# A decode attention block: key and value tiles of four heads and 8 MB in three buffers, in place of two heads and 4 MB in five

## The chip, the cores and the metric

The kernel runs on one core of a Trainium2 chip. The metric is the device time of one execution in microseconds, as the median of several runs. Beside it there is a profile of one execution, with the span from the first to the last instruction.

## The reference

A block with adaptive layer norm: attention of one new token per sequence over a cache of 4096 keys and values in 32 heads, then a feed-forward part. All arrays are float32; the two caches have 268 MB each.

```python
B, D, H, Sk, Dh, F = 4, 512, 32, 4096, 128, 1792
mod = (silu(c) @ w_mod).reshape(4, 6, 1, -1)            # shifts, scales and gates sa, ca, ga, sb, cb, gb
h = layernorm(x) * (1 + ca) + sa
q = (h @ wq) split into 32 heads                        # B, H, 1, Dh
p = softmax(einsum("bhqd,bhkd->bhqk", q, k_cache) * Dh ** -0.5)
o = einsum("bhqk,bhkd->bhqd", p, v_cache)
x = x + ga * (o.reshape(B, 1, H * Dh) @ wo)
h = layernorm(x) * (1 + cb) + sb
return x + gb * (silu(h @ w1) @ w2)
```

## The kernel before

The work on the caches goes in N = 64 steps `n`, one for each of 16 pairs of heads (`t`) and each of 4 sequences (`b`). A step has one K tile and one V tile of 4 MB: two heads (`HP` = 2), each spread over 64 partitions (`HALF`), with 64 consecutive cache rows (`NJ`), that is 32 KB in one piece of the cache, on each partition. All large loads are issued by SyncE (SP) through `fetch` (L71), in program order, into five buffers of 32 KB per partition (pool `kv`, `bufs=5`) that are reused in turn. The order of instructions on each engine is that of the program (a manual schedule). A load waits on SP until the last reader of its buffer's old tile is done, and the loads behind it wait with it.

Step n, by engine:

- `mult` (L216): GpSimd multiplies the first `NA` = 24 of the 64 rows of a partition by the query, in place, with the query's copy `qw` in SBUF; VectorE does the other 40 with the query `qb` in PSUM.
- `red` (L221), VectorE: sums each row's 128 products to a score; first the 40 rows, then the 24 of GpSimd.
- `rowmax` (L225), VectorE; `bmax` (L229), a transpose on TensorE that spreads the maxima over the partitions; `negmax` (L236), VectorE, per head.
- `softexp` (L247), ScalarE: exponentials, one instruction per head, written into the zero-padded tile `pz` at distances of 32 columns, and their sum into `rs`.
- `pv` (L260), TensorE: 16 products of four cache rows at a time with the exponentials, added up in PSUM tile `po`. Each is issued in two passes (x2 in the instruction counts), and so are the other float32 products.

Once in four steps, `make_qb` (L202, L210) spreads the queries of a head pair over the partitions by products with `ident` columns, and `finish_a` and `finish_b` (L269 to L285) copy `po` to SBUF, gather the values by 16 products with columns of `sel`, and divide by the sum of the exponentials; the result goes into `oz`.

Before the steps come the modulation (`mods`, L146), the first layer norm and the queries (L186), whose weights `wm` and `wq` pass through the same five buffers. After the steps come the output projection (`project`, L294), the second layer norm (L161 to L173), and the feed-forward products (L352, L362). Their weights `wo`, `w1` and `w2` follow the last tiles through the buffers, cut into several loads. In the last four steps the loads stand in an order of their own, written by hand: K61, K62, K63, V61, V62, the first half of `wo`, V63, the second half of `wo`, `w1`, `w2`.

Of the kernel before, what the change touches and what calls it, by code (L numbers as in the profile page):

```python
# [17 lines left out]
def kernel(  # L18
# [20 lines left out]
    HP = 2  # L39
    HALF = P // HP  # L40
# [3 lines left out]
    NG = NJ // JJ  # L44
    NK = D // P
    NI = F // P
    FG = F // G
    NA = 24
# [3 lines left out]
    NP = 3  # L52

    const = ctx.enter_context(tc.tile_pool(name="const", bufs=1))
    kv = ctx.enter_context(tc.tile_pool(name="kv", bufs=5))
# [7 lines left out]
    wmv = wm.rearrange("(p k) n -> p k n", p=P)  # L63
    wqv = wq.rearrange("(p k) n -> p k n", p=P)
    wov = wo.rearrange("(t p j) n -> p t j n", p=P, j=HP)
    w1v = w1.rearrange("(p k) f -> p k f", p=P)
    w2v = w2.rearrange("(p i) d -> p i d", p=P)
# [31 lines left out]
    wmt = [load(f"wm{i}", [P, 2, 6 * D], wmv[:, 2 * i : 2 * i + 2, :]) for i in range(2)]  # L99
    wqt = [load(f"wq{i}", [P, 2, H * Dh], wqv[:, 2 * i : 2 * i + 2, :]) for i in range(2)]  # L100
# [4 lines left out]
    blk = const.tile([P, P], F32, name="blk")  # L105
    nc.vector.memset(blk, 0.0)
    for i in range(HP):
        nc.vector.memset(blk[HALF * i : HALF * (i + 1), HALF * i : HALF * (i + 1)], 1.0)
# [12 lines left out]
    oz = const.tile([P, NT, HP, W], F32, name="oz")
    nc.gpsimd.memset(oz, 0.0)

    def silu2(dst, src, n):
        t = work.tile([P, FG], F32, tag="silu", name="silu", bufs=1)
        nc.scalar.activation(t[:, :n], src, AF.Tanh, scale=0.5)
        nc.vector.scalar_tensor_tensor(dst, t[:, :n], 1.0, src, op0=ALU.add, op1=ALU.mult)

    def transposed(src, m, name):
        d = const.tile([P, m, W], F32, name=name)  # L130
        nc.vector.transpose(d, src.rearrange("p (c k) -> p k c", k=m))  # L131
        return d

    cs = const.tile([P, P], F32, name="cs")
    silu2(cs, cg, P)
    csT = transposed(cs, NK, "csT")
    mod = const.tile([P, 6, P], F32, name="mod")
    sa, ca1, ga, sb, cb1, gb = (mod[:, i, :] for i in range(6))

    def mods(i, m):  # L140
# [34 lines left out]
    mods(0, 2)  # L175
    hg = const.tile([P, P], F32, name="hg")
    layernorm_mod(hg, xg, sa, ca1)
    hT = transposed(hg, NK, "hT")
    mods(2, 4)

    CW = 4 * Dh
    pq = [psum([P, CW], "q", 2) for _ in range(2)]
    for k in range(NK):
        for ch in range(H * Dh // CW):
            i, g = divmod(ch, G)
            nc.tensor.matmul(  # L186
                pq[i][W * g : W * (g + 1), :], hT[:, k, :], wqt[k // 2][:, k % 2, ch * CW : (ch + 1) * CW],
                start=k == 0, stop=k == NK - 1,
            )
    qs = const.tile([P, 2, CW], F32, name="qs")  # L190
    for i in range(2):
        nc.scalar.activation(qs[:, i, :], pq[i], AF.Copy, scale=SCALE)

    qb, qw = {}, {}

    def make_qb(t):
        p = psum([P, B, Dh], "q", 2)
        for b in range(B):
            for i in range(HP):
                ch, u = divmod(HP * t + i, CW // Dh)  # L200
                j, g = divmod(ch, G)
                nc.tensor.matmul(  # L202
                    p[HALF * i : HALF * (i + 1), b, :],
                    ident[:, W * g + b : W * g + b + 1].to_broadcast([P, HALF]),
                    qs[:, j, u * Dh : (u + 1) * Dh],
                    start=True, stop=True,
                )
        qb[t] = p
        qw[t] = work.tile([P, B, Dh], F32, tag="qw", name=f"qw{t}")
        nc.scalar.activation(qw[t], p, AF.Copy)  # L210

    sc, nm, po, rs, sm = {}, {}, {}, {}, {}

    def mult(eng, src, n, lo, hi):
        t, b = divmod(n, B)
        eng.tensor_mul(  # L216
            kt[n][:, lo:hi, :], kt[n][:, lo:hi, :], src[t][:, b : b + 1, :].to_broadcast([P, hi - lo, Dh])
        )
# [4 lines left out]
    def rowmax(n):  # L223
        nm[n] = work.tile([P, 1], F32, tag="rm", name=f"rm{n}", bufs=3)
# [7 lines left out]
    def negmax(n):  # L232
        t = work.tile([P, 1], F32, tag="nm", name=f"nm{n}", bufs=3)
        for i in range(HP):
            h = slice(HALF * i, HALF * (i + 1))
            nc.vector.tensor_reduce(t[h], nm[n][h, h], axis=AX.X, op=ALU.max, negate=True)  # L236
        nm[n] = t

    def softexp(n):
        t, b = divmod(n, B)  # L240
        if b == 0:
            rs[t] = work.tile([P, B], F32, tag="rs", name=f"rs{t}", bufs=3)
        o = W // 2 - JJ
        for i in range(HP):
            h = slice(HALF * i, HALF * (i + 1))
            w = pz[n % NP][h, : NG * W].rearrange("p (g w) -> p g w", w=W)
            nc.scalar.activation(  # L247
                w[:, :, o + i * W // 2 : o + i * W // 2 + JJ],
                sc[n][h].rearrange("p (g j) -> p g j", j=JJ),
                AF.Exp, bias=nm[n][h], accum_out=rs[t][h, b : b + 1],  # L250
            )

    def pv(n):
        t, b = divmod(n, B)
        if b == 0:
            po[t] = psum([P, JJ * Dh], "po", 2)
        o = W // 2 - JJ - JJ * b
        for j in range(NG):
            g = j % G
            nc.tensor.matmul(  # L260
                po[t][W * g : W * (g + 1), :],
                pz[n % NP][:, j * W + o : (j + 1) * W + o],
                vt[n][:, JJ * j : JJ * (j + 1), :].rearrange("p j d -> p (j d)"),
                start=(b == 0 and j < G), stop=(b == B - 1 and j >= NG - G),
            )

    def finish_a(t):
        o = work.tile([P, JJ, Dh], F32, tag="o", name="o")
        nc.vector.tensor_copy(o, po[t].rearrange("p (j d) -> p j d", j=JJ))  # L269
        d = psum([P, 1 + HP, B], "small", 1)  # L270
        nc.tensor.matmul(d[:, 0, :], blk, rs[t], start=True, stop=True)
        for i in range(HP):
            for r in range(HP):
                for j in range(JJ):
                    s = i * W // 2 + j
                    nc.tensor.matmul(  # L276
                        d[HALF * i : HALF * (i + 1), 1 + r, :], o[:, j, r::HP], sel[:, s : s + JJ * (B - 1) + 1 : JJ],
                        start=j == 0, stop=j == JJ - 1,
                    )
        sm[t] = d  # L280

    def finish_b(t):
        rd = work.tile([P, 1, B], F32, tag="rd", name="rd")
        nc.vector.reciprocal(rd, sm[t][:, 0:1, :])
        nc.vector.tensor_mul(oz[:, t, :, :B], sm[t][:, 1 : 1 + HP, :], rd.to_broadcast([P, HP, B]))  # L285

    accp = psum([P, P], "acc", 1)
    wot = []

    def project(lo, hi):  # L290
        for t in range(lo, hi):
            for r in range(HP):
                for g in range(G):
                    nc.tensor.matmul(  # L294
                        accp[W * g : W * (g + 1), :], oz[:, t, r, :],
                        wot[t // NH][:, t % NH, r, g * P : (g + 1) * P],
                        start=(t == 0 and r == 0), stop=(t == NT - 1 and r == HP - 1),
                    )
# [98 lines left out]
```

## Time and profile before

| | |
|---|---|
| runs | 1332.4, 1333.32, 1333.3 us; median 1333.3 us |
| profiled execution | 1334.54 us, its span 1332.5 us |
| granted TensorE clock, mean | 0.656 |
| bytes moved by DMA | 567.87 MB, mean 426 GB/s over the span |
| busy: VectorE, TensorE, GpSimd, ScalarE | 976.2, 504.9, 435.2, 75.7 us |

The profile is of one execution. A busy TensorE counts pipelined products that overlap, so the sum of their durations is larger than its busy time. DMA share is the mean busy share of the core's 16 DMA engines; in short stretches it can come out somewhat above 1, since a packet's time and bytes are counted where the packet lies by its start or end. In lines of groups, the columns are line, engine, operation, tiles written and read with their shapes, count, busy time in us and mean ns of one, and then the idle time before them with what ended it. In lines of the timeline and of the chain, the first number is the start in us, the second the duration. In the stretches view the columns are the stretch, its length, the busy time of TensorE, its weight load, VectorE, ScalarE and GpSimd, each with a count of instructions in brackets, and last the granted clock, the DMA share and GB/s.

### The profile page before, as it was taken

The page shows a single profiled execution, that of the slowest core. Times are in us where ns is not written, and L with a number is a line of the kernel's source. Part 1 is how long each engine was busy: PE and PEld are TensorE (multiplying, and loading weights), DVE is VectorE, ACT ScalarE, POOL GpSimd, SP SyncE. Part 2 cuts the span into 40 slices and gives each one's busy share as a digit, 9 for nine tenths or more (in the row PEclk, how much of TensorE's full clock was granted, in tenths as well). Part 3 has the DMA queues.
Part 4 walks back from the last instruction along what each step waited for, and adds up shares of the span by engine and source line. Part 5 has one row for each costly group of instructions (what it writes and reads, how often), then busy time and mean ns, then how long its engine had stood idle before and what let it go on. Part 6 is the DMA issues. An engine that isn't in the chain of part 4 may idle for free.

```text
span 1332.5 us, 8833 instructions
## 1 busy us (share of the span) xinstructions
PE 504.9 (38%) x3576; PEld 181.2 (14%) x3576; DVE 976.2 (73%) x468; ACT 75.7 (6%) x289; POOL 435.2 (33%) x79
## 2 busy tenths in 40 slices
PE   3244324433442533443343233334333333433157
PEld 2011101110110111101011110101111011101024
DVE  1487787788778778777877877777787787778851
ACT  1100000000000000000000000000000000000000
POOL 1244234324323423432442343243234234324600
PEclk9666677666656666656666676576666556666677
DMA  9999999999999999999999999999999999999997
GB/s 407 427 430 433 426 436 428 429 435 426 433 432 429 433 427 435 430 430 432 427 435 429 428 434 429 432 430 431 432 429 430 430 432 432 431 428 433 431 414 288
DMA packets 22376, 567.87 MB, mean 426 GB/s; under 512 B 2448, under 2 KB 2496, under 8 KB 5056
## 3 DMA queue, kind: packets, MB, share of 16 engines
q1 hardware_dynamic: 22160, 567.29, 99.3%
q8 instruction: 28, 0.46, 0.1%
q14 instruction: 12, 0.10, 0.0%
q0 software_dynamic: 128, 0.01, 0.0%
q10 hardware_dynamic: 48, 0.01, 0.0%
HBM read 567.30 MB, written 0.01 MB: 426 GB/s over the span
## 4 chain that ended last, share of the span: by engine, by line
DMA 48%; DVE 35%; PE 10%; issue 4%; ACT 2%; DVEq 0%; ACTq 0%
DMA k<-in_A_k_cache_dram 45%; DVE sc L221 20%; DVE k L216 13%; PE po L260 8%; DMA v<-in_A_v_cache_dram 2%; ACT pz L247 2%; PE mx L229 1%; DMA wm<-in_w_mod_dram 1%; DVE o L269 1%; DVE rm L225 1%; DVE nm L236 1%; PE acc L294 0%; PE po L362 0%; PE q L352 0%; DVE oz L285 0%
## 5 line engine op out<-in xcount | busy, mean ns | idle before, releaser
L216 POOL TENSOR_TENSOR k<-k,qw 128x3072 f32<-128x3072 f32 x64 | 429.7, 6715 | 827.9 <-DMA k<-in_A_k_cache_dram 786.7
L221 DVE TENSOR_REDUCE sc<-k 128x40 f32<-128x5120 f32 (+1 forms) x128 | 560.8, 4413 | 5.2
L216 DVE TENSOR_TENSOR k<-k,q 128x5120 f32<-128x5120 f32 x64 | 351.2, 5488 | 245.9 <-DMA k<-in_A_k_cache_dram 188.2
L260 PE MATMUL po<-v,pz 128*32 128x512 f32 x2048 | 371.5, 892 | 103.0 <-ACT pz L247 77.1
L229 PE MATMUL mx<-ident,rm 128*128 128x128 f32 x64 | 28.5, 445 | 641.4 <-DVE rm L225 641.4
L260 PEld LDWEIGHTS po<-v,pz 128*32 128x32 f32 x2048 | 82.6, 155 | 349.0 <-issue 256.3
L247 ACT ACTIVATE pz<-sc,nm 64x64 f32<-64x64 f32 x128 | 44.2, 345 | 1054.1 <-DVE nm L236 1052.5
L229 PEld LDWEIGHTS mx<-ident,rm 128*128 128x128 f32 x64 | 11.6, 181 | 676.2 <-issue 648.2
L236 DVE TENSOR_REDUCE nm<-mx 64x1 f32<-64x64 f32 x128 | 28.4, 222 | 45.9 <-PE mx L229 43.9
L276 PE MATMUL small<-sel,o 128*64 128x4 f32 x512 | 43.0, 231 | 46.6 <-DVE o L269 46.6
L276 PEld LDWEIGHTS small<-sel,o 128*64 128x64 f32 x512 | 41.6, 190 | 48.0 <-DVE o L269 48.0
L247 ACT ACTIVATION_READ_ACCUMULATOR pz<-sc,nm 64x1 f32 x128 | 23.6, 185 | 0.0
L269 DVE COPY o<-po 128x512 f32<-128x512 f32 x16 | 11.0, 684 | 16.2 <-PE po L260 16.2
L202 PE MATMUL q<-qs,ident 128*64 128x128 f32 x256 | 17.5, 279 | 0.0
L225 DVE TENSOR_REDUCE rm<-sc 128x1 f32<-128x64 f32 x64 | 14.1, 220 | 2.2
L202 PEld LDWEIGHTS q<-qs,ident 128*64 128x64 f32 x256 | 13.6, 136 | 14.5 <-issue 14.5
L210 ACT ACTIVATE qw<-q 128x512 f32<-128x512 f32 x16 | 9.6, 597 | 105.5 <-PE q L202 105.5
L146 PE MATMUL q<-wm,csT 128*32 128x128 f32 x192 | 7.5, 322 | 17.2 <-DVE csT L131 13.5
L186 PE MATMUL q<-wq,hT 128*32 128x512 f32 x64 | 10.1, 790 | 9.5 <-DMA wq<-in_A_wq_dram 9.5
L294 PE MATMUL acc<-wo,oz 128*32 128x128 f32 x256 | 11.7, 369 | 0.4 <-DMA wo<-in_A_wo_dram 0.4
L294 PEld LDWEIGHTS acc<-wo,oz 128*32 128x32 f32 x256 | 11.2, 154 | 0.7 <-issue 0.6
L146 PEld LDWEIGHTS q<-wm,csT 128*32 128x32 f32 x192 | 6.2, 129 | 17.9 <-DVE csT L131 13.5
(57 smaller groups left out, 63.8 us busy)
## 6 DMA issues: line engine op xcount, KB each, us to landing
k<-in_A_k_cache_dram SPq DMA_DIRECT2D x64, 4096.0 KB, 36.0
v<-in_A_v_cache_dram SPq DMA_DIRECT2D x64, 4096.0 KB, 30.3
wq<-in_A_wq_dram SPq DMA_DIRECT2D x2, 4096.0 KB
wm<-in_w_mod_dram SPq DMA_DIRECT2D x2, 3072.0 KB, 10.1
wo<-in_A_wo_dram SPq DMA_DIRECT2D x1, 4096.0 KB
wo<-in_A_wo_dram SPq DMA_DIRECT2D x1, 2048.0 KB
w<-in_B_w_dram SPq DMA_DIRECT2D x1, 2048.0 KB, 23.7
w<-in_B_w_dram SPq DMA_DIRECT2D x1, 1792.0 KB
```

The costliest lines, as they stand in the source:

```text
L146: nc.tensor.matmul(p[W * g : W * (g + 1), u, :], csT[:, k, :], wmt[k // 2][:, k % 2, o : o + P], start=k == 0, stop=k == NK - 1,)
L202: nc.tensor.matmul(p[HALF * i : HALF * (i + 1), b, :], ident[:, W * g + b : W * g + b + 1].to_broadcast([P, HALF]), qs[:, j, u * Dh : (u + ...
L216: eng.tensor_mul(kt[n][:, lo:hi, :], kt[n][:, lo:hi, :], src[t][:, b : b + 1, :].to_broadcast([P, hi - lo, Dh]))
L221: nc.vector.tensor_reduce(sc[n][:, lo:hi], kt[n][:, lo:hi, :], axis=AX.X, op=ALU.add)
L225: nc.vector.tensor_reduce(nm[n], sc[n], axis=AX.X, op=ALU.max)
L229: nc.tensor.transpose(p, nm[n].to_broadcast([P, P]), ident)
L236: nc.vector.tensor_reduce(t[h], nm[n][h, h], axis=AX.X, op=ALU.max, negate=True)
L247: nc.scalar.activation(w[:, :, o + i * W // 2 : o + i * W // 2 + JJ], sc[n][h].rearrange("p (g j) -> p g j", j=JJ), AF.Exp, bias=nm[n][h], ...
L260: nc.tensor.matmul(po[t][W * g : W * (g + 1), :], pz[n % NP][:, j * W + o : (j + 1) * W + o], vt[n][:, JJ * j : JJ * (j + 1), :].rearrange ...
L269: nc.vector.tensor_copy(o, po[t].rearrange("p (j d) -> p j d", j=JJ))
L276: nc.tensor.matmul(d[HALF * i : HALF * (i + 1), 1 + r, :], o[:, j, r::HP], sel[:, s : s + JJ * (B - 1) + 1 : JJ], start=j == 0, stop=j == ...
L294: nc.tensor.matmul(accp[W * g : W * (g + 1), :], oz[:, t, r, :], wot[t // NH][:, t % NH, r, g * P : (g + 1) * P], start=(t == 0 and r == 0 ...
```

## The change

A step now takes four heads (`HP` = 4) of one sequence, on 32 partitions each (`QW`): N = 32 steps with a K and a V tile of 8 MB, with 128 cache rows and 64 KB in one piece per partition. There are three buffers of 64 KB per partition. Of the 128 rows GpSimd multiplies 56 (`NA`), VectorE 72.

- Loads: K(n+1) is issued at the head of step n, V(n+1) behind `softexp(n)`; near the end the order is K30, K31, V30, V31, `wo`, `w1` and `w2`. `wm` and `wq` are one load each, and `wo` has runs of 8 KB. Small tiles of the start (among them `cg`, `qs` and the selecting matrix `zsel`) share the first buffer with `wm`, and small tiles of the end share the last one with `w1` and `w2`.
- Queries: eight products with shifted views of `zsel` put the 32 pairs of head group and sequence into one tile `qn`; `make_qb` runs in each step: ScalarE masks `qn` by a column of `sel`, one product with the block matrix `blk` spreads it, ScalarE copies it to SBUF.
- Exponentials: one ScalarE instruction for all four heads, in place; then two GpSimd products with the head mask `hm` spread them into `pz` (two half tiles in place of three whole ones).
- `negmax`: a maximum per head, a product with the negative head mask, and a sum.
- `pv`: 32 products; `po` serves two sequences, so there are two `po` tiles per head group.
- Values: `gather` masks `po` by `jm` on VectorE and adds up four products with the selecting matrix `spick`, after two and after four sequences; `norm` forms the reciprocal sums on TensorE and VectorE; `spread` divides, transposes on VectorE and copies into `oz`.
- End: the projection is interleaved with the last `gather` and `spread`, and small products `busy` without use stand on TensorE between the products of the feed-forward part.

The core of the diff:

```diff
-    HP = 2
-    HALF = P // HP
+    HP = 4
+    QW = P // HP
...
-    NA = 24
+    NA = 56
...
-    kv = ctx.enter_context(tc.tile_pool(name="kv", bufs=5))
+    kv = ctx.enter_context(tc.tile_pool(name="kv", bufs=3))
...
+    def load(dst, cache, name, n):
+        t, b = divmod(n, B)
+        dst[n] = Slot(f"{name}{n}").take(NJ, Dh)
+        src = cache[b, HP * t : HP * (t + 1)].rearrange("h (p j) d -> (h p) j d", p=QW)
+        nc.sync.dma_start(dst[n], src)
...
-    wov = wo.rearrange("(t p j) n -> p t j n", p=P, j=HP)
+    wov = wo.rearrange("(t p r) n -> p t r n", p=P, r=R)
...
+    s0 = Slot("wm")
+    wmt = s0.take(NK, 6 * D)
+    cg, cs, hg0, sa, ca1 = (s0.take(P) for _ in range(5))
...
+    qs = s0.take(2, CW)
+    zsel = s0.take(ZB + P)
...
+    pqn = psum([P, Dh], "mx", 2)
+    for i in range(2):
+        for u in range(HP):
+            o = ZB - QW * u - G * B * i
+            nc.tensor.matmul(
+                pqn, zsel[:, o : o + P], qs[:, i, u * Dh : (u + 1) * Dh],
+                start=i + u == 0, stop=i == 1 and u == HP - 1,
+            )
+    qn = const.tile([P, Dh], F32, name="qn")
+    nc.scalar.activation(qn, pqn, AF.Copy)
...
+    def make_qb(n):
+        m = work.tile([P, Dh], F32, tag="lnu", name=f"qm{n}", bufs=1)
+        nc.scalar.activation(m, qn, AF.Copy, scale=sel[:, n : n + 1])
+        p = psum([P, Dh], "q", 2)
+        nc.tensor.matmul(p, blk.rearrange("p i x -> p (i x)"), m, start=True, stop=True)
+        qb[n] = p
+        qw[n] = work.tile([P, Dh], F32, tag="qw", name=f"qw{n}")
+        nc.scalar.activation(qw[n], p, AF.Copy)
...
+        m = work.tile([P, HP], F32, tag="hx", name=f"hx{n}")
+        nc.vector.tensor_reduce(m, nm[n].rearrange("p (i x) -> p i x", i=HP), axis=AX.X, op=ALU.max)
+        nc.vector.tensor_mul(m, m, hn)
+        nm[n] = work.tile([P, 1], F32, tag="nm", name=f"nm{n}")
+        nc.vector.tensor_reduce(nm[n], m, axis=AX.X, op=ALU.add)
...
+        nc.scalar.activation(sc[n], sc[n], AF.Exp, bias=nm[n], accum_out=rs[t][:, b : b + 1])
+        for h in range(2):
+            nc.gpsimd.tensor_mul(
+                pz[h][:, : HG * W].rearrange("p (g x) -> p g x", g=HG)[:, :, E:].rearrange("p g (i j) -> p g i j", i=HP),
+                sc[n][:, HG * JJ * h : HG * JJ * (h + 1)].rearrange("p (g j) -> p g j", j=JJ)
+                .unsqueeze(2).to_broadcast([P, HG, HP, JJ]),
+                hm.unsqueeze(1).unsqueeze(3).to_broadcast([P, HG, HP, JJ]),
+            )
...
+    def gather(t, q):
+        o = work.tile([P, JJ, Dh], F32, tag="o", name="o", bufs=1)
+        nc.vector.tensor_mul(
+            o, po[t, q].rearrange("p (j d) -> p j d", j=JJ), jm.unsqueeze(2).to_broadcast([P, JJ, Dh])
+        )
+        if q == 0:
+            od[t] = psum([P, Dh], "od", 1)
+        for j in range(JJ):
+            nc.tensor.matmul(
+                od[t], spick[:, 2 - 2 * q : 2 - 2 * q + P], o[:, j, :],
+                start=(q == 0 and j == 0), stop=(q == 1 and j == JJ - 1),
+            )
...
+    def spread(t):
+        on = work.tile([P, R, QW], F32, tag="lnu", name="on", bufs=1)
+        nc.vector.tensor_scalar(
+            on, od[t].rearrange("p (x r) -> p r x", r=R), rd[t][:, 1:2], None, op0=ALU.mult
+        )
+        ot = work.tile([P, R, W], F32, tag="ot", name="ot", bufs=1)
+        nc.vector.transpose(ot, on)
+        nc.vector.tensor_copy(oz[:, t], ot[:, :, :B])
...
     for n in range(N):
         t, b = divmod(n, B)
-        if n + 1 < N - 3:
+        if n + 1 < N - 1:
             load_k(n + 1)
-            load_v(n + 1)
...
+        elif n == N - 2:
+            load_v(n)
         else:
-            load_v(n)
-            wot.append(load("wo1", [P, NH, HP, D], wov[:, NH:], 0, NH // 2, 3 * NH // 4, NH - 1, NH))
+            so = Slot("wo")
+            wot = so.take(NT, R, D)
+            fetch(wot, wov, 0, NT // 2, NT - 2, NT - 1, NT)
...
         mult(nc.gpsimd, qw, n, 0, NA)
         mult(nc.vector, qb, n, NA, NJ)
+        if n + 1 < N:
+            make_qb(n + 1)
         red(n, NA, NJ)
+        if n and b == 0:
+            gather(t - 1, 1)
+        if b == 2:
+            gather(t, 0)
         red(n, 0, NA)
+        if n and b == 0:
+            spread(t - 1)
         rowmax(n)
         bmax(n)
         negmax(n)
         softexp(n)
+        if n < N - 3:
+            load_v(n + 1)
+        elif n == N - 3:
+            load_k(N - 1)
+        elif n == N - 2:
+            load_v(N - 1)
+        else:
+            s2 = Slot("w12")
+            w1t = s2.take(NK, F)
+            w2t = s2.take(NI, D)
+            fetch(w1t, w1v, 0, 2, 3, 4)
+            fetch(w2t, w2v, 0, 4, 8, 11, 13, 14)
+        if b == B - 1:
+            norm(t)
         pv(n)
+    project(0, NT // 2)
+    gather(NT - 1, 1)
+    project(NT // 2, NT - 1)
+    spread(NT - 1)
+    project(NT - 1, NT)
...
+    busy(4)
     layernorm_mod(hg, x1, sb, cb1)
-    h2T = transposed(hg, NK, "h2T")
+    transposed(h2T, hg, NK)
+    busy(5)
```

More of the change, by code (lines that the diff above doesn't have):

```diff
@@ L98 @@
         nc.gpsimd.dma_start(xg[W * g : W * g + B, :], xr[:, g * P : (g + 1) * P])
-    wmt = [load(f"wm{i}", [P, 2, 6 * D], wmv[:, 2 * i : 2 * i + 2, :]) for i in range(2)]
-    wqt = [load(f"wq{i}", [P, 2, H * Dh], wqv[:, 2 * i : 2 * i + 2, :]) for i in range(2)]
+    nc.sync.dma_start(wmt, wmv)
+    s1 = Slot("wq")
+    wqt = s1.take(NK, H * Dh)
+    nc.sync.dma_start(wqt, wqv)
     load_k(0)
@@ L104 @@
     make_identity(nc, ident)
[L105 to L108, printed above, removed]
+    i4 = ident.rearrange("p (i x) -> p i x", i=G)
     epst = const.tile([P, 1], F32, name="epst")
@@ L111 @@
     sel = const.tile([P, W], F32, name="sel")
-    nc.vector.tensor_add(sel, ident[:, 0:W], ident[:, W : 2 * W])
-    for g in range(2, G):
-        nc.vector.tensor_add(sel, sel, ident[:, W * g : W * (g + 1)])
+    nc.vector.tensor_reduce(sel, ident.rearrange("p (g x) -> p x g", g=G), axis=AX.X, op=ALU.add)
     avg = const.tile([P, G, W], F32, name="avg")
@@ L117 @@
         nc.vector.tensor_scalar(avg[:, g, :], sel, 1.0 / G, None, op0=ALU.mult)
-    pz = [const.tile([P, NG * W + W // 2], F32, name=f"pz{i}") for i in range(NP)]
+    hm = const.tile([P, HP], F32, name="hm")
+    nc.vector.tensor_reduce(hm, i4, axis=AX.X, op=ALU.add)
+    hn = const.tile([P, HP], F32, name="hn")
+    nc.vector.tensor_scalar(hn, hm, -1.0, None, op0=ALU.mult)
+    jm = const.tile([P, JJ], F32, name="jm")
+    nc.vector.tensor_reduce(jm, ident.rearrange("p (k j) -> p j k", j=JJ), axis=AX.X, op=ALU.add)
@@ new lines @@
+    xm = const.tile([P, B], F32, name="xm")
+    nc.vector.tensor_copy(xm, sel[:, 0:B])
+    pad = const.tile([P, 1], F32, name="pad")
+    nc.vector.tensor_reduce(pad, sel[:, B:W], axis=AX.X, op=ALU.add)
+    nc.vector.tensor_add(xm[:, 0:1], xm[:, 0:1], pad)
+    blk = const.tile([P, HP, QW], F32, name="blk")
+    nc.vector.tensor_copy(blk, hm.unsqueeze(2).to_broadcast([P, HP, QW]))
+    spick = const.tile([P, P + 2], F32, name="spick")
+    nc.vector.memset(spick, 0.0)
+    ia = ident.rearrange("p (g a i j) -> p a i g j", g=G, a=2, i=HP)
@@ L119 @@
+    sp3 = spick[:, 2:].rearrange("p (i x) -> p i x", i=HP)
+    for a in range(2):
+        nc.vector.tensor_reduce(sp3[:, :, a], ia[:, a], axis=AX.XY, op=ALU.add)
+    pz = [const.tile([P, HG * W + E], F32, name=f"pz{i}") for i in range(2)]
     for t in pz:
         nc.gpsimd.memset(t, 0.0)
[L121 to L140, printed above, removed]
+    oz = const.tile([P, NT, R, B], F32, name="oz")
+    nc.vector.memset(zsel, 0.0)
@@ new lines, with silu2, transposed @@
+    nc.vector.tensor_copy(zsel[:, ZB:P].rearrange("p (g x) -> p g x", g=G), i4[:, :, :B])
+    def silu2(dst, t, src):
+        nc.scalar.activation(t, src, AF.Tanh, scale=0.5)
+        nc.vector.scalar_tensor_tensor(dst, t, 1.0, src, op0=ALU.add, op1=ALU.mult)
+    def transposed(dst, src, m):
+        nc.vector.transpose(dst, src.rearrange("p (c k) -> p k c", k=m))
+    silu2(cs, tmp, cg)
+    transposed(csT, cs, NK)
+    mod = const.tile([P, 4, P], F32, name="mod")
+    ga, sb, cb1, gb = (mod[:, i, :] for i in range(4))
@@ L141, in mods @@
+    def mods(dsts, i):
         p = psum([P, 4, P], "q", 2)
-        for u in range(m):
+        for u in range(len(dsts)):
             for k in range(NK):
@@ L223, in rowmax @@
     def rowmax(n):
[L224 removed]
+        nm[n] = work.tile([P, 1], F32, tag="rm", name=f"rm{n}")
         nc.vector.tensor_reduce(nm[n], sc[n], axis=AX.X, op=ALU.max)
@@ L241, in softexp @@
         if b == 0:
[L242 to L250, printed above, removed]
+            rs[t] = work.tile([P, B], F32, tag="rs", name=f"rs{t}")
+        nc.scalar.activation(sc[n], sc[n], AF.Exp, bias=nm[n], accum_out=rs[t][:, b : b + 1])
[5 more added lines that the diff above has]
+                hm.unsqueeze(1).unsqueeze(3).to_broadcast([P, HG, HP, JJ]),
             )
@@ L263, in pv @@
                 vt[n][:, JJ * j : JJ * (j + 1), :].rearrange("p j d -> p (j d)"),
-                start=(b == 0 and j < G), stop=(b == B - 1 and j >= NG - G),
+                start=(a == 0 and j < G), stop=(a == 1 and j >= NG - G),
             )
[L267 to L285, printed above, removed]
+    od = {}
+    def gather(t, q):
[10 more added lines that the diff above has]
+            )
@@ new lines, with norm @@
+    rd = {}
+    def norm(t):
+        p = psum([P, B], "mx", 2)
+        nc.tensor.matmul(p, blk.rearrange("p i x -> p (i x)"), rs[t], start=True, stop=True)
+        m = work.tile([P, B], F32, tag="dx", name="dx")
+        nc.vector.tensor_mul(m, p, xm)
+        rd[t] = work.tile([P, 2], F32, tag="rd", name="rd")
+        nc.vector.tensor_reduce(rd[t][:, 0:1], m, axis=AX.X, op=ALU.add)
+        nc.vector.reciprocal(rd[t][:, 1:2], rd[t][:, 0:1])
+    def spread(t):
[6 more added lines that the diff above has]
+        nc.vector.tensor_copy(oz[:, t], ot[:, :, :B])
@@ L332, with busy @@
         softexp(n)
-        if n == N - 1:
-            w1t = load("w1", [P, NK, F], w1v, 0, 2, 3, 4)
-            w2t = load("w2", [P, NI, D], w2v, 0, 8, 12, 13, 14)
-            project(0, NH)
-        pv(n)
-        if b == 1 and t + 1 < NT:
-            make_qb(t + 1)
-    finish_a(NT - 1)
-    finish_b(NT - 1)
-    project(NH, NT)
-    x1 = const.tile([P, P], F32, name="x1")
+        if n < N - 3:
[12 more added lines that the diff above has]
+            norm(t)
+        pv(n)
+    project(0, NT // 2)
[3 more added lines that the diff above has]
+    project(NT - 1, NT)
+    idle = psum([P, P], "q", 2)
+    def busy(m):
+        for _ in range(m):
+            nc.tensor.matmul(idle, ident, qn, start=True, stop=True)
+    x1, hg, y = (s2.take(P) for _ in range(3))
+    h2T, hid, th, hidT = s2.take(NK, W), s2.take(FG), s2.take(FG), s2.take(NI, W)
     nc.vector.tensor_mul(x1, ga, accp)
     nc.vector.tensor_add(x1, x1, xg)
+    busy(4)
     layernorm_mod(hg, x1, sb, cb1)
-    h2T = transposed(hg, NK, "h2T")
+    transposed(h2T, hg, NK)
+    busy(5)
     ph = psum([P, FG], "q", 2)
@@ L355 @@
             )
-    hid = const.tile([P, FG], F32, name="hid")
-    silu2(hid, ph, FG)
-    hidT = transposed(hid, NI, "hidT")
+    busy(6)
+    silu2(hid, th, ph)
+    transposed(hidT, hid, NI)
     pf = psum([P, P], "po", 2)
```

123 lines of the change are left out of this document (48 added, 75 removed).

## The prediction

> **What bounds the kernel now.** First the page's engine totals, the 40-slice strip and the DMA lines, then the two longest waits of SP.
>
> ```profile
> span 1332.5 us, 8833 instructions
> PE 504.9 (38%) x3576; PEld 181.2 (14%) x3576; DVE 976.2 (73%) x468; ACT 75.7 (6%) x289; POOL 435.2 (33%) x79
> DMA  9999999999999999999999999999999999999997
> DMA packets 22376, 567.87 MB, mean 426 GB/s; under 512 B 2448, under 2 KB 2496, under 8 KB 5056
> q1 hardware_dynamic: 22160, 567.29, 99.3%
> k<-in_A_k_cache_dram SPq DMA_DIRECT2D x64, 4096.0 KB, 36.0
> v<-in_A_v_cache_dram SPq DMA_DIRECT2D x64, 4096.0 KB, 30.3
> ...
> SPq L71 <- DVE rm L225: 719.5, 63, 15.5
> SPq L71 <- PE po L260: 464.9, 61, 9.5
> ```
>
> The DMA engines are busy in every slice, 99.3% of the span on SP's queue alone. VectorE has 73% of the span, no other engine more than 38%. A K tile lands 36.0 us after its issue, while one tile's data passes in about 9.7 us, so three transfers or more always stand in the queue. What SP waits for (719.5 us on VectorE, 464.9 us on TensorE) is only that queue being full. So I look for what makes the DMA engines' own work shorter, and then at the two ends of the span, where the queue can run dry.
>
> Packets, from the stretches view. The second row is almost all from `wo`, whose runs are 4 KB, the third likewise; the first is K and V alone, in 32 KB runs. Its last two columns are DMA share and GB/s.
>
> ```profile
> 60.00:1260.00 1200.00, 443.52 (x2764) 146.43 (x2764) 930.23 (x417) 64.45 (x264) 418.99 (x63) 0.64 1.00 431
> 1276.00:1279.00 3.00, 2.12 (x12) 0.74 (x16) 2.89 (x2) 0.00 (x0) 0.00 (x0) 0.66 1.01 406
> 1301.00:1304.00 3.00, 3.00 (x20) 0.84 (x16) 0.00 (x0) 0.00 (x0) 0.00 (x0) 0.50 1.05 424
> ```
>
> The 22160 packets add up as one packet for each contiguous run: 16384 of K and V (128 transfers x 128 partitions), 3456 of the weights, 2304 completion writes (144 loads x 16 engines), 16 for the output's data and completions. No run up to 32 KB is cut. Rate over share is 431 GB/s for 32 KB runs, and 406/1.01 = 402 and 424/1.05 = 404 for 4 KB ones. With 16 engines a 32 KB packet takes 32768 x 16 / 431 = 1216 ns, a 4 KB one 65536 / 403 = 162.6 ns. A line through both has a slope of 0.03675 ns per byte and 12 ns per packet that don't depend on size (11 to 13 by the rounding of the shares).
>
> **The change part by part.**
>
> *K and V in 64 KB runs.* Bytes stay; if the 64 KB run is one packet, it takes 65536 x 0.03675 + 12 = 2420 ns in place of 2 x 1216. An engine now handles 16384/16 = 1024 such packets; 512 fall away, 512 x 12 = **-6.1 us** (-5.6 to -6.7). Bound from the other side: 0, if the run is cut in two. I take one packet, by the count above. 64 fewer transfers also save 64 completion writes per engine, between 0 and 12 ns each: **-0.4 us**. `wo` goes from 4 KB to 8 KB runs: 64 packets less per engine, -0.8 us; `wm` in one piece and two extra cuts of `w2` cancel.
>
> The Trainium skill (SBUF — State Buffer, The DMA setup-cost knee) puts one DMA at 2 us plus bytes over 436 GB/s; by that, 64 DMAs fewer would save 128 us and the sum would be near 1205 us. The trace disagrees: K and V run at 431 GB/s without gaps, so that fixed cost lies under the queued transfers.
>
> *Three buffers.* Counting allocations, K(n+1) takes the place of V(n-1), and V(n+1) that of K(n), so V(n+1) can be issued only when K(n) has been reduced. Does the queue hold? Rows of instructions by form, then the first and the last regular K tile from the chain, and two groups of `pv` from the timeline:
>
> ```profile
> L216 POOL TENSOR_TENSOR k<-k,qw 128x3072 f32<-128x3072 f32 x64 | 429.7, 6715 | 827.9 <-DMA k<-in_A_k_cache_dram 786.7 <-issue 41.2
> L260 PE MATMUL po<-v,pz 128*32 128x512 f32 x2048 | 371.5, 892 | 103.0 <-ACT pz L247 77.1 <-DMA v<-in_A_v_cache_dram 21.9 <-issue 4.0
> L216 DVE TENSOR_TENSOR k<-k,q 128x5120 f32<-128x5120 f32 x64 | 351.2, 5488 | 245.9 <-DMA k<-in_A_k_cache_dram 188.2 <-issue 57.6
> L221 DVE TENSOR_REDUCE sc<-k 128x40 f32<-128x5120 f32 x64 | 350.9, 5483 | 5.2
> L221 DVE TENSOR_REDUCE sc<-k 128x24 f32<-128x3072 f32 x64 | 213.9, 3343 | 0.0
> L236 DVE TENSOR_REDUCE nm<-mx 64x1 f32<-64x64 f32 x128 | 28.4, 222 | 45.9 <-PE mx L229 43.9
> L269 DVE COPY o<-po 128x512 f32<-128x512 f32 x16 | 11.0, 684 | 16.2 <-PE po L260 16.2
> 48.74 5.50 DVE k L216
> 1237.86 5.50 DVE k L216
> 669.55 5.24 PE L260 MATMUL po<-v,pz 128*32 128x512 f32 x32 [1.30 <-ACT pz L247]
> 1298.39 6.54 PE L260 MATMUL po<-v,pz 128*32 128x512 f32 x32 [3.46 <-DMA v<-in_A_v_cache_dram]
> ```
>
> K tiles arrive (1237.86 - 48.74)/61 = 19.49 us apart now, so the new ones 2 x 19.49 - 0.2 = 38.8. Per tile, VectorE multiplies 72 x 128 = 9216 elements (5488 x 9216/5120 = 9.9 us) and reduces them (9.9), then reduces the 7168 of GpSimd's part (3343 x 7168/3072 = 7.8). GpSimd multiplies 7168 in 15.7 us, done before the last reduce wants them at 19.8. K(n) is free 27.6 us after it lands (28.4 with the `o` multiply, 0.7 us, in two of four tiles). V(n+1) has to start about 37 us after K(n) lands, when K(n+1) is through: **9 us to spare**. The rest of VectorE's work (maximum, its spread over heads, norm, gather, spread) is some ten instructions of 0.2 to 0.7 us; with its waits VectorE stays near 32 of 38.8 us. K(n+2) waits for `pv(n)`: exponentials at 30 us, two GpSimd spreads of 256 elements (15.7 x 256/7168 = 0.6 us each; even ten times that leaves room), 64 matmuls, twice the 6.5 us of now, done by 45 of 57 us. Cost 0, hidden under DMA. On SP's queue the order V(n+1), K(n+2) is the order in which they come free, so no transfer is held behind another's wait. The new ScalarE and TensorE work of `make_qb` (two copies, one product per tile) is hidden too: ScalarE is at 6%.
>
> *Start.* `v0` now waits until `qs` and `zsel`, which share the buffer of `wm`, have been read.
>
> ```profile
> 29.30 3.64 PE L186 MATMUL q<-wq,hT 128*32 128x512 f32 x32 [3.44 <-DMA wq<-in_A_wq_dram]
> 38.96 6.50 PE L186 MATMUL q<-wq,hT 128*32 128x512 f32 x32 [6.02 <-DMA wq<-in_A_wq_dram]
> 45.39 1.09 PE L202 MATMUL q<-qs,ident 128*64 128x128 f32 x16
> ```
>
> `wq` is complete at 39 as now, but all 64 matmuls come behind it: 7.3 us at the pace of the first row, 13 at that of the second, say 10; the two ScalarE copies 1.5, sixteen 128x128 products about 2.5; `v0` is issued near 53 (50 to 57). `k0`, 9.7 us longer, lands at 58.4 and leaves the engines near 57. **0** (to +1).
>
> *End.* The order is now V30, V31, `wo`, `w1`/`w2`; `wo` needs the buffer of K31. Counting from K30's landing, VectorE frees K31 at about 2 x 28.4 = 57, when V31, the third transfer after, is just through at 58: a gap of 0 to 3 us, **+1**. Chain and timeline of the tail:
>
> ```profile
> 1304.99 0.70 DVE o L269
> 1305.74 1.88 PE small L276 x32
> 1307.62 5.34 PE acc L294 x128
> 1312.98 0.29 DVE L345 TENSOR_TENSOR x<-mod,acc 128x128 f32<-128x128 f32 x1 [4.95 <-PE acc L294]
> 1316.96 4.96 PE q L352 x32
> 1321.94 0.55 ACT silu L126
> 1324.16 4.97 PE po L362 x112
> ```
>
> Now the last V lands at 1298.4 (the `pv` row above) and 34.1 us of chain follow. Afterwards 4.19 MB less stand before the last V (the first half of `wo` moves behind it): 4.19 MB / 403 GB/s = -10.4 us, and with -6.5 from the packets it lands at 1281.5. Then: wait for exponentials and spread 2; `pv` 64 matmuls, 13 at the slow pace, 10 if the clock rises midway (as in the 669.55 row against the 1298.39 row), take 10.5; first half of the projection 5.3; gather 1.9; second half 5.3, its `spread` beside it; `x1` to `h2T` 4.0 (the extra products fill TensorE's wait, 0 to 1 more); `L352` 5.0; SiLU and transpose 2.2; last product 5.0; output 3.4. Sum **44.6** (43 to 51). Loads allow no less than 1 + 8.39/0.415 + 7.34/0.425 + 3.6 = 42 (rates between the 403 of 4 KB and 431 of 32 KB). Span 1281.5 + 44.6 = 1326.1.
>
> **Sum.** 1326.1 against 1332.5, -6.4 us. The profiled execution took 1334.5, the median of the runs is 1333.3; 1333.3 - 6.4 = 1326.9, and half of the start's possible +1 makes **1327.4**.
>
> **The rivals.**
>
> *The run is cut, no gain (0.14).* The 6.1 us stay; with 44.6 of tail the span is 1332.2 to 1333, about 1333.7. Against it: every shorter run is one packet, and the line through sizes has nothing that bends.
>
> *The tail eats it (0.07).* `pv` and both projections at the slow pace, 51 us in all: 1281.5 + 51 = 1332.5, the time 1333.3. For it: in the 1298.39 row the slow pace lasts for all 6.54 us; against it: TensorE is busy without a break behind it.
>
> *The queue runs dry (0.06, slower).* One mechanism: V(n+1) waits for K(n), with two full loads queued at best instead of three. It decides from 37 us between landing and release; each microsecond above is paid 32 times. If VectorE and GpSimd came to 38 us, 1327 + 32 = 1359. For it: before, K's buffer had two more tiles to be freed; against it the 27.6 us above, made of rows that vary by under 1%.
>
> *Longer runs read worse (0.05, slower).* The 128 partitions' sources lie 64 KB apart instead of 32; were packets 1% slower, K and V's 1246 us (64 x 2 x 9.73) would cost 12 us: 1339. The rows are against it: 4 KB and 32 KB runs fit one line, though no row has a pitch above 32 KB.
> The Trainium skill (DMA: Bandwidth & Descriptors, Latency and other measured facts) reports copies slowing at large power-of-two row pitches, 207 against 214 GB/s at 512 KiB and worse above. By that loss, 3.3%, the sum would be near 1368; no run here shows a pitch so large.
>
> **How the numbers follow.** Forecast 0.68, with 1323 to 1331. A change under 0.2% (1330.6 to 1336) can't be told from none. Faster: nearly all of the forecast (0.65) and 0.01 of the cut run; same: 0.03 of the forecast, 0.10 of the cut run, 0.05 of the tail; slower: the last two rivals and what is left, 0.16. The range 1322 to 1335 holds the first three cases, 0.89 in all less their edges; low is a microsecond under the tail's 42 us floor with all savings at their upper bounds, high the cut run with 1.3 us more of tail.
>
> **What would show it.** Right: half the packets, none cut, with 433 GB/s at full share between 100 and 1250; K tiles 38.8 us apart; SP's waits for K(n) ending about 28 us after landing; a strip of nines. A gap of about 1 us before `wo`, and the last `pv` starting near 1283. Wrong: 431 GB/s with more packets than 12,500; idle DMA share in the middle; GpSimd's spread above 5 us; or a tail beyond 51 us.

## The result and the profile after

The changed kernel takes 1325.51 us (median of 4 runs, 1325.08 to 1325.72) against 1333.31 us before: a ratio of 0.9944, 95% interval 0.9931 to 0.9956, or 7.8 us less. The forecast was 1327.4. The profiled execution has a span of 1323.6 us, 8.9 us under that of before. In later and larger sets of 10 to 20 runs the kernel before had medians of 1332.7 to 1332.9 us; by these the gain is 7.2 to 7.4 us, and times of different sets can be compared to about 0.6 us.

The page of the changed kernel, lines of totals, DMA and queue:

```profile
span 1323.6 us, 7040 instructions
PE 401.4 (30%) x2998; PEld 144.7 (11%) x2998; DVE 923.2 (70%) x332; ACT 44.6 (3%) x146; POOL 533.4 (40%) x109
DMA  9999999999999999999999999999999999999988
DMA packets 11968, 567.75 MB, mean 429 GB/s; under 512 B 1393, under 2 KB 1441, under 8 KB 2081
q1 hardware_dynamic: 11760, 567.29, 99.3%
```

The packets on SP's queue fall from 22160 to 11760. That is one for each 64 KB run: 8192 for K and V, and no run is cut. DMA still sets the time: 99.3% again, a strip of nines, and now two eights at its end. The stretches view gives the middle, in which K and V alone pass, and a stretch near the end (last columns: granted clock, DMA share, GB/s):

```profile
60.00:1260.00 1200.00, 342.77 (x2145) 112.39 (x2145) 889.30 (x275) 32.38 (x122) 517.48 (x94) 0.61 1.00 433
...
1275.00:1280.00 5.00, 0.45 (x1) 0.18 (x1) 4.27 (x5) 0.00 (x0) 0.00 (x0) 0.50 0.38 139
```

433 GB/s in place of 431, at the same share. And from 1275 to 1280 us, ahead of `wo`, the view has a DMA share of only 0.38, which would be 3.1 us of idle engines on average. That overstates it: packets of 64 KB last 2.4 us and reach across the edges of so short a stretch. The packet records of the trace (start, length and size of each packet), cut at the edges, give 2.6 us. Rows of one regular step from the timeline (start, duration, engine, line):

```profile
640.13 9.76 DVE L251 TENSOR_TENSOR k<-k,q 128x9216 f32<-128x9216 f32 x1 [9.46 <-DMA k<-in_A_k_cache_dram]
640.14 15.35 POOL L251 TENSOR_TENSOR k<-k,qw 128x7168 f32<-128x7168 f32 x1 [7.68 <-DMA k<-in_A_k_cache_dram]
649.92 17.28 DVE L256 TENSOR_REDUCE sc<-k 128x72 f32<-128x9216 f32 x2
667.23 0.33 SPq L90 DMA_DIRECT2D v<-in_A_v_cache_dram  x1
669.44 1.18 POOL L280 TENSOR_TENSOR pz<-sc,hm 128x256 f32<-128x256 f32 x2 [13.95 <-ACT sc L278]
670.10 8.62 PE L296 MATMUL po<-v,pz 128*32 128x512 f32 x64
678.79 0.33 SPq L90 DMA_DIRECT2D k<-in_A_k_cache_dram  x1
678.84 9.76 DVE L251 TENSOR_TENSOR k<-k,q 128x9216 f32<-128x9216 f32 x1 [8.24 <-DMA k<-in_A_k_cache_dram]
```

VectorE starts on a K tile as it lands, at 640.13, frees it 27.1 us later, and SP issues the next V in the same instant; VectorE then idles 8.2 us until the next K lands, 38.7 us after the first. GpSimd's two spreads take 1.18 us together. The end, first rows of the chain (start, duration), then three rows of the timeline:

```profile
1261.19 17.29 DVE sc L256 x2
...
1278.93 0.50 SPq L82
1279.48 20.20 DMA wo<-in_A_wo_dram
1299.70 19.45 DMA w<-in_B_w_dram
1319.19 0.95 PE po L427 x24
```

```profile
1281.45 8.44 PE L296 MATMUL po<-v,pz 128*32 128x512 f32 x64
1303.43 0.29 DVE L408 TENSOR_TENSOR w<-mod,acc 128x128 f32<-128x128 f32 x1 [5.46 <-PE acc L345]
1319.19 0.90 PE L427 MATMUL po<-w 128*32 128x128 f32 x24 [0.60 <-DMA w<-in_B_w_dram]
```

Before, the chain behind the last V went through compute alone. Now it goes through the loads: VectorE frees K31's buffer at 1278.5, `wo` starts behind that, `w1` and `w2` follow without a break, and the last product waits for the last piece of `w2` (0.60 us). The kernel ends 4.4 us after that piece. V31 isn't through when the buffer comes free: by the packet records its last 16 packets end one after the other from 1275.8 to 1279.7, so some engines stand idle from 1275 on, while `wo` can't be queued yet.

### The profile page after: what moved, and what is told of

The parts are those of the page before. It is cut to its first block, busy times and chain, and to the rows that moved or that the text cites. A ratio compares the mean times of both kernels' runs of the same rounds, so it can differ in the third digit from the quotient of the medians.

```text
span 1323.6 us, 7040 instructions
## 1 busy us (share of the span) xinstructions
PE 401.4 (30%) x2998; PEld 144.7 (11%) x2998; DVE 923.2 (70%) x332; ACT 44.6 (3%) x146; POOL 533.4 (40%) x109
## 3 DMA queue, kind: packets, MB, share of 16 engines
q1 hardware_dynamic: 11760, 567.29, 99.3%
## 4 chain that ended last, share of the span: by engine, by line
DMA 31%; issue 30%; POOL 25%; PE 9%; DVE 4%; SPq 0%; POOLq 0%; ACT 0%; DVEq 0%
DMA k<-in_A_k_cache_dram 25%; POOL k L251 24%; PE po L296 8%; DMA wq<-in_A_wq_dram 3%; DVE sc L256 3%; DMA wo<-in_A_wo_dram 2%; DVE k L251 1%; DMA w<-in_B_w_dram 1%; POOL pz L280 1%; PE q L220 1%; PE mx L230 0%; PE po L427 0%; POOLq L280 0%; DVE o L307 0%; DVE rm L260 0%
## 5 line engine op out<-in xcount | busy, mean ns | idle before, releaser
L251 POOL TENSOR_TENSOR k<-k,qw 128x7168 f32<-128x7168 f32 x32 | 491.4, 15357 | 289.5 <-DMA k<-in_A_k_cache_dram 263.6
L256 DVE TENSOR_REDUCE sc<-k 128x72 f32<-128x9216 f32 x64 | 554.2, 8681 | 1.1
L251 DVE TENSOR_TENSOR k<-k,q 128x9216 f32<-128x9216 f32 x32 | 312.1, 9754 | 308.9 <-DMA k<-in_A_k_cache_dram 308.9
L296 PE MATMUL po<-v,pz 128*32 128x512 f32 x2048 | 297.8, 747 | 56.8 <-POOL pz L280 45.8
L280 POOL TENSOR_TENSOR pz<-sc,hm 128x256 f32<-128x256 f32 x64 | 37.9, 613 | 458.2 <-ACT sc L278 458.2
L264 PE MATMUL mx<-ident,rm 128*128 128x128 f32 x32 | 14.5, 454 | 520.1 <-DVE rm L260 520.1
L313 PE MATMUL od<-o,spick 128*128 128x128 f32 x128 | 32.3, 432 | 290.2 <-DVE o L307 290.2
L313 PEld LDWEIGHTS od<-o,spick 128*128 128x128 f32 x128 | 27.7, 319 | 293.3 <-DVE o L307 293.1
L278 ACT ACTIVATE sc<-sc,nm 128x128 f32<-128x128 f32 x32 | 12.8, 401 | 884.7 <-DVE nm L272 884.7
L243 PE MATMUL q<-qm,blk 128*128 128x128 f32 x64 | 15.6, 326 | 1.5 <-ACT qm L241 1.5
L220 PE MATMUL q<-wq,wm 128*32 128x512 f32 x64 | 8.7, 701 | 9.5 <-DMA wq<-in_A_wq_dram 9.5
L166 DVE SCALAR_TENSOR_TENSOR wm<-wm 128x128 f32<-128x128 f32 x1 | 0.3, 293 | 12.5 <-ACT wm L165 12.5
```

What stands on the lines that cost most here:

```text
L220: nc.tensor.matmul(pq[i][W * g : W * (g + 1), :], hT[:, k, :], wqt[:, k, ch * CW : (ch + 1) * CW], start=k == 0, stop=k == NK - 1,)
L243: nc.tensor.matmul(p, blk.rearrange("p i x -> p (i x)"), m, start=True, stop=True)
L251: eng.tensor_mul(kt[n][:, lo:hi, :], kt[n][:, lo:hi, :], src[n].unsqueeze(1).to_broadcast([P, hi - lo, Dh]))
L256: nc.vector.tensor_reduce(sc[n][:, lo:hi], kt[n][:, lo:hi, :], axis=AX.X, op=ALU.add)
L264: nc.tensor.transpose(p, nm[n].to_broadcast([P, P]), ident)
L278: nc.scalar.activation(sc[n], sc[n], AF.Exp, bias=nm[n], accum_out=rs[t][:, b : b + 1])
```

## The experiments

### Runs of 32 and of 16 KB with everything else as changed

```diff
-        nc.sync.dma_start(dst[n], src)
+        for lo in range(0, NJ, NJ // c):        # c = 2: e1_32k, c = 4: e2_16k
+            nc.sync.dma_start(dst[n][:, lo : lo + NJ // c], src[:, lo : lo + NJ // c])
```

> The changed kernel with each 8 MB tile of K and V loaded as two transfers of 4 MB, so in runs of 32 KB again; buffers, steps and all compute as in the changed kernel. Packet theory (12 ns per packet, whatever its size, and 9 to 12 ns per completion): 512 more packets and 64 more completions per engine, 6.1 + 0.6 = 6.7 us more than the changed kernel, about 1332.2 us, 431 GB/s in the middle. Rival, the gain comes from the larger step and the rearranged end and not from the runs: unchanged at 1325.5.

> As before, but four transfers of 2 MB per tile, runs of 16 KB. Packet theory: 1536 more packets and 192 more completions per engine than the changed kernel, 18.4 + 1.9 = 20.3 us, about 1345.8 us, and 427 GB/s in the middle; the step from 32 KB to 16 KB is twice that from 64 KB to 32 KB. Rival, a cost of 64 KB or 32 KB runs that isn't linear in the count of packets: steps that don't stand 1 to 2. Rival, larger step only: 1325.5.

Measured: 1330.17 us for e1_32k (11 runs, 1329.94 to 1331.24) and 1337.97 for e2_16k (5 runs, 1337.96 to 1338.95): 4.7 and 12.5 us over the changed kernel, where 6.7 and 20.3 were expected. The middle of e1_32k, and then of e2_16k, in the stretches view:

```profile
60.00:1260.00 1200.00, 337.68 (x2161) 112.02 (x2165) 884.46 (x275) 32.37 (x122) 507.62 (x94) 0.61 1.00 431
```

```profile
60.00:1260.00 1200.00, 343.64 (x2144) 112.88 (x2144) 876.05 (x270) 31.87 (x120) 504.08 (x91) 0.61 1.01 428
```

So the run's length does set the rate (433, 431, 428 GB/s), and the rival that gives all to the larger step falls. (Each halving also doubles the transfers and their completion writes; the runs price both together. A completion write lasts 9 ns and comes once per 8 packets.) But the price per packet was too high. With 16 KB runs the share stands at 1.01 over 1200 us: packets of one engine overlap a little, so a part of each packet's own 12 ns is hidden under its neighbour.

The packet records say how much. In this stretch packets of 64, 32 and 16 KB last 2423, 1218 and 615 ns on average, and all packets together come to 1.0017, 1.0032 and 1.0065 of the time: an overlap of 4 ns per packet at each size. 12 - 4 + 9/8 is an estimate of 9 ns for a packet with its part of a completion.

The steps of 4.7 and 7.8 us also don't stand 1 to 2; the next experiments tell why.

### `wo` into a buffer that is free earlier

```diff
-            so = Slot("wo")
+            so = slots["v", N - 2]              # the buffer of V30
+            so.at = 0
             wot = so.take(NT, R, D)
```

> The changed kernel with wo put into the buffer of V30, which TensorE frees about 10 us before it is needed, in place of that of K31, which VectorE frees after V31 has passed; w1 and w2 take K31's. The stretch without DMA ahead of wo (share 0.38 from 1275 to 1280 us) goes. If the mean idle time of the engines counts, the loads end 3 us earlier and the time falls to about 1322.5. If only the slowest engine counts (its last packet of V31 ends at about 1279.5, as the first of wo starts), nothing is gained: 1325.3, with the loads spread over more time at their end.

Measured: 1323.58 us (5 runs, 1323.51 to 1323.73), 1.9 us under the changed kernel and 0.9928 of the kernel before (0.9916 to 0.9941): the fastest version here. It lies between the two theories. Its stretch ahead of `wo`, and rows of its chain:

```profile
1275.00:1280.00 5.00, 0.45 (x1) 0.18 (x1) 4.26 (x5) 0.00 (x0) 0.00 (x0) 0.50 0.87 369
```

```profile
1279.35 29.36 DMA w<-in_B_w_dram
1308.76 1.00 PE q L419 x8
...
1311.11 0.55 ACT w L166
...
1313.34 4.98 PE po L429 x112
```

The share ahead of `wo` rises from 0.38 to 0.87 in the view; by the packet records no idle time is left there, so all 2.6 us are gone. The last packet of `w2` ends at 1317.0 in place of 1319.2. Of 2.6 us of mean idle time, 2.2 came back in the loads, which bears out the first theory for them, and 1.8 in the span. 0.4 are lost to compute, which sets the end again: behind the last piece of `w1` (1308.7) the chain has no load, and the last product runs 4.98 us without a wait for `w2`.

The same edit with 32 KB runs closes the count:

> e3_wo_in_v30 with each tile in two loads, so in runs of 32 KB, and without the gap ahead of wo. Theory, a price of 9.4 ns per packet that is the same between 64, 32 and 16 KB, and the gap costing e1_32k as much as the changed kernel: 512 x 9.4 = 4.8 us more than e3_wo_in_v30, 1328.4. Rival, the first halving costs less than the second: e1_32k's 4.7 us hold with a smaller gap in it, and 1329 to 1330 comes out.

Measured: 1328.59 us (6 runs, 1328.46 to 1328.61). Without the gap, 64, 32 and 16 KB give 1323.58, 1328.59 and 1337.97: steps of 5.0 us for 512 packets and 9.4 us for 1024, so 9.8 and 9.2 ns per packet with its part of a completion. In e2_16k the DMA share stays at 0.98 to 1.02 from the last V to `wo`, so it had no gap to lose. The changed kernel's gap costs 1.9 us, and that of e1_32k 1.6; the uneven steps above came from there.

What is left of the unevenness lies at the end: compute ends the first two kernels and the wait for `w2` the third. The loads themselves end at 1317.0, 1322.0 and 1331.8, steps of 5.0 and 9.8 us, which stand 1 to 2. For the middle alone, the first 503 MB of K and V, the packet records give 1162.0, 1167.4 and 1176.7 us, which is 11 and 9.6 ns per packet. So the price is some 10 ns, known to about 1.

### The price per packet in the kernel before

```diff
-        kt[n] = load(f"k{n}", [P, NJ, Dh], src)
+        kt[n] = load(f"k{n}", [P, NJ, Dh], src, 0, NJ // 2, NJ)      # and vt[n] likewise
```

> The kernel before with each 4 MB tile in two loads of 2 MB, so in runs of 16 KB: 1024 more packets and 128 more completions per engine. By the price that e2_16k against e3_wo_in_v30 gives (14.4 us for 1536 packets and 192 completions, 9.4 ns per packet with its part of a completion): 9.6 us more, about 1342.3. By 12 ns per packet and 9 per completion, as the packets' own durations say: 13.4 us more, 1346.

Measured: 1343.12 us (5 runs, 1342.9 to 1345.4) against 1332.82 of the kernel before on the same chip, ratio 1.0081 (1.0067 to 1.0094): 10.3 us for 1024 packets, 10 ns each with their part of a completion (8.7 to 12.2 by the interval). So packets have about the same price with 4 MB tiles and five buffers: it lies nearer to the 9.4 ns of the other kernels than to the 13 (12 and an eighth of 9) of the durations.

### How much room three buffers leave

```diff
-    NA = 56
+    NA = 16            # with wo in V30's buffer
```

> e3_wo_in_v30 with GpSimd's share cut from 56 to 16 of 128 rows. VectorE multiplies and reduces 112 rows, 2 x 15.2 us, and then 16, 2.2: K(n) is free 32.6 us after it lands, in place of 27.1, and VectorE works 35 to 36 us of a 38.8 us step. If the queue holds until 37 us, as forecast: 433 GB/s and K tiles 38.8 us apart in the middle, and only the end is later, since the last exponentials come 11 us later: the loads were ahead of the chain there by some 6, so about 1328.5 us. If three buffers run dry earlier than worked out: 1 us or more for each of 31 steps, over 1355 us.

Measured: 1329.39 us (10 runs, 1328.63 to 1330.19). The timeline of this kernel, three rows of the same step as above:

```profile
640.21 15.09 DVE L252 TENSOR_TENSOR k<-k,q 128x14336 f32<-128x14336 f32 x1 [4.12 <-DMA k<-in_A_k_cache_dram]
672.64 0.33 SPq L91 DMA_DIRECT2D v<-in_A_v_cache_dram  x1
678.91 15.09 DVE L252 TENSOR_TENSOR k<-k,q 128x14336 f32<-128x14336 f32 x1 [2.91 <-DMA k<-in_A_k_cache_dram]
```

The K tile is freed after 32.4 us in place of 27.1, and the next one still lands 38.7 us behind the first, at 678.9 in both kernels. The middle passes at 433 GB/s as before, and the last V is through at 1279.7 in both, so the 5.8 us against e3_wo_in_v30 lie behind it. So the room forecast for three buffers is there, for at least 5 us; where it ends wasn't tried, since VectorE itself would be full at 38.8 us.

### The extra products at the end

```diff
-        for _ in range(m):
+        for _ in range(0 * m):
             nc.tensor.matmul(idle, ident, qn, start=True, stop=True)
```

> The changed kernel without the 15 extra products that keep TensorE busy at the end. If the end is set by the last loads, as the waits of the last product for w2 say: no change, within 0.5 us of 1325.5. If it is set by TensorE's pace: the feed-forward products take 4.9 us each as before the change, in place of 3.4 and 3.9, and 1 to 2.5 us are lost.

Measured: 1325.72 us (5 runs, 1325.2 to 1326.23), unchanged. The feed-forward product falls back to its old pace (first row, 4.74 us), and what is lost there comes out of the waits for `w2` (second row: 0.36 us in place of 0.60):

```profile
1307.69 4.74 PE L417 MATMUL q<-w 128*32 128x448 f32 x32 [1.38 <-DVE w L169]
1319.34 1.07 PE L427 MATMUL po<-w 128*32 128x128 f32 x24 [0.36 <-DMA w<-in_B_w_dram]
```

### What else e1_32k has over the kernel before

With equal runs, e1_32k is still 2.5 us faster than the kernel before (ratio 0.9981, 0.9972 to 0.999).

```diff
         elif n == N - 2:
-            wot.append(load("wo0", [P, NH, HP, D], wov[:, :NH]))
+            load_v(N - 1)
         else:
-            load_v(n)
+            wot.append(load("wo0", [P, NH, HP, D], wov[:, :NH]))
...
-    project(NH, NT)
+    project(0, NT)                              # and no project(0, NH) ahead of pv(63)
```

> The kernel before, with V63 loaded ahead of the first half of wo in place of behind it, and the whole projection behind the last products with V. Runs, step and buffers as before. e1_32k has the same 32 KB runs and is still 2.5 us faster than the kernel before. Theory, the end: there 34.1 us of chain follow V63 while the loads behind it need 27.6 + 3.6; with V63 10 us earlier the loads set the end: 2 to 2.9 us less, about 1330.2. Rival, the 2.5 us come from the 8 MB step (fewer transfers and instructions, wo in 8 KB runs): 1332.7, unchanged.

Measured: 1332.3 us (11 runs, 1331.42 to 1333.5), ratio 0.9997 (0.9988 to 1.0006): no change that can be told. Both kernels were profiled once more:

> The kernel before, profiled once more, since its executions spread over 1331.3 to 1334.4 us and the profile shown had 1334.54. If the end makes the spread (TensorE's pace behind V63): loads end at the same time, about 1325 us, and a shorter execution has a shorter chain behind V63. If the loads make it: V63 lands at another time.

> e6_before_v63_first, profiled once more for the same reason: its profile had 1331.6 us, its median 1332.3. If the loads set its end, the last products wait for w2 again; if the chain does, they don't, and the time is near 1332.3 or above.

The kernel before took 1332.76 us this time, its variant 1333.45. From the timelines: V63's products and the last product in the kernel before (again), then the last product in the variant's first and in its second profile:

```profile
1297.98 5.34 PE L260 MATMUL po<-v,pz 128*32 128x512 f32 x32 [4.04 <-DMA v<-in_A_v_cache_dram]
1322.46 4.92 PE L362 MATMUL po<-w,hidT 128*32 128x128 f32 x112 [2.29 <-DVE hidT L131]
```

```profile
1324.59 1.74 PE L361 MATMUL po<-w,hidT 128*32 128x128 f32 x48 [0.46 <-DMA w<-in_B_w_dram]
```

```profile
1321.94 6.12 PE L361 MATMUL po<-w,hidT 128*32 128x128 f32 x112 [3.34 <-DMA w<-in_B_w_dram]
```

The profile shown ahead of the prediction was a late one of its kernel: there the products with V63 took 6.54 us, here 5.34, and the span is 1330.8 in place of 1332.5. The variant shows both ends: in its first profile the last product waits for `w2` (0.46 us) and the span is 1329.7; in the second it starts when a load lands, then takes 6.12 us at TensorE's slow pace, and the span is 1331.5. So the end by compute is worth 1 to 2 us in some executions and nothing in others, and it doesn't carry the 2.5 us. The loads end at 1325.0 to 1325.4 in all four profiles of the kernel before and its variant, and at 1323.8 in e1_32k.

The packet records show where most of it lies. 15360 packets of K and V, 960 per engine, pass in 1169.1 us in these four profiles, and in 1167.4 us in e1_32k and e8_32k_wo_in_v30, though all have 32 KB: on average they last 1218.9 ns and 1217.6. So 1.7 us are won in the middle, where neither `wo` nor the order of the last loads plays a part. Why packets of the same size are shorter there stays open. Fewer instructions to fetch (0.38 MB on their queue in place of 0.46) are a candidate that was not tried; their own packets last 2.3 and 1.9 us per engine in all, so directly they can account for 0.4. What `wo` in 8 KB runs gains (1024 packets less, 64 per engine, at 9.4 to 12 ns 0.6 to 0.8 us by estimate) was not tried alone either.

## Why the prediction was right, point by point

- *DMA bounds, and a 64 KB run is one packet:* right; 11760 packets, 433 GB/s, and the rate falls with each halving of the run. The line of packet times was drawn through two sizes, so by itself it couldn't have shown a bend; packets of 64 and 16 KB, at 2423 and 615 ns, now lie on it (2420 and 614).
- *-6.1 us for 512 packets and -0.4 for completions:* the step was right and its size too large. The chip gives 5.0 us for both together (e8_32k_wo_in_v30 against e3_wo_in_v30). The 12 ns were read from how long packets last, and packets overlap by 4: 9.2 to 9.8 ns count over the whole kernel, completion included. Among the weights, `wq` in one load was left out and `w2` has one extra cut, not two: 128 packets less where the forecast had them cancel, some 0.1 us.
- *Three buffers cost nothing:* right. K(n) was forecast to be free after 27.6 us and is after 27.1; 5 us more cost nothing in the middle. K tiles were forecast 38.8 us apart and are 38.7. GpSimd's spreads were forecast at 0.6 us each and take 0.59. `pv` was put at 13 us at the slow pace and takes 8.6 here.
- *Start, 0 (to +1):* right. K0 was to land at 58.4, and VectorE starts on it at 58.0; `v0` is issued at 47.3, earlier than the 53 forecast: it took the buffer of `wq`, free once the products of L220 were done, and `k1` that of `wm`.
- *A gap of 0 to 3 us ahead of `wo`, +1:* right in its place, and in its cause as e3_wo_in_v30 shows; 2.6 us in mean idle time and 1.9 in what it costs. Counted from K30's landing (1222.2), K31's buffer is free at 56.3 and V31 through at 57.5, for 57 and 58 in the forecast. What the forecast didn't have is that engines finish their parts of V31 at different times; those that finish early make the gap.
- *End, 44.6 us behind V31, by compute:* the number was near and the reason was not; that it was near is luck. Less the 2 us of waiting, the forecast had 42.6 us from the last `pv` on, starting at 1283.5; `pv` starts at 1281.45 and 42.2 us follow. But the loads set them. TensorE's products were shorter than forecast (`pv` 8.4 for 10.5, first half of the projection 3.7 for 5.3), so compute was done before the loads. These took longer than the floor that the forecast gave them: 44.1 us from the start of `wo`, where its terms without the gap come to 41, above all `w1` and `w2` with 19.5 us for 17.3. *The tail eats it* wanted 51 us and falls.
- *The sum:* -6.4 forecast (-5.9 in the number given), -7.8 measured. 4.7 are the runs, with the gap in both kernels (5.0 without it); 2.5 are there with equal runs too, 1.7 of them in the middle from a cause that stays open; 0.6 is the kernel before, slower in this set than in the later ones. The forecast had -6.5 for the packets, 1.5 too much, and nothing for the rest together, where some 2.5 more were won. So the mechanism of the forecast carries about two thirds of the gain, and that the sum came within 2 us is in part luck: two errors offset each other.

*The run is cut* falls by the count of packets, *the queue runs dry* by e5_na16, *longer runs read worse* by the 433 GB/s: at a pitch of 64 KB nothing is lost. The Trainium skill (DMA: Bandwidth & Descriptors, Latency and other measured facts) reports a loss for copies between HBM tensors at pitches of 512 KiB and more; no run here has such a pitch. The Trainium skill (SBUF — State Buffer, The DMA setup-cost knee) fits one DMA with 2 us plus its bytes over 436 GB/s. In the full queue of these kernels the 2 us don't show: e2_16k has 192 more transfers than the changed kernel and takes 12.5 us more, not 384.

## What to carry to other kernels

Where the DMA engines are busy throughout, count the packets: here each costs some ten nanoseconds on its engine beside its bytes, so longer contiguous runs pay (up to 64 KB in these runs) even when bytes, share and queue stay the same. By the argument of the three buffers, tested here with 5 us less room and not to its limit, a tile may grow until its buffers leave just enough room between the release of one and the end of the transfers queued. Work that room out from the step's own rows, as a time from landing to release against the time the queue still holds. At the end of such a kernel, give each load the buffer that comes free first: 1.9 us went with one load waiting for a reduction while another buffer had been free for 9 us.

## What was not expected of the hardware

The durations of packets add up to more than the time that passes: with 16 KB runs the DMA share is 1.01 over 1200 us, and 12 ns of a packet's duration cost some 10 with a part of a completion. And a share read in a short stretch can overstate a gap: where packets last 2.4 us, the view of 5 us ahead of `wo` had 3.1 us of idle engines and the packet records 2.6. In e3_wo_in_v30 the view still has a share of 0.87 there, where the records show no idle engine. Last, packets of 32 KB passed 1.7 us sooner over 1169 us in one kernel than in another, in every profile of each.
